# Clustered attention and an MLP on one core: the written order of all steps, its buffers and semaphores, made anew

## The chip, the cores and the metric

The kernel runs on one core of a Trainium2 chip. The metric is the time of one execution on the device in microseconds; the median of three runs is given, and beside it one execution that the hardware profiler recorded.

## The reference

q, k and v are float32 of shape 4 x 8 x 768 x 64 (batch, heads, sequence, head dimension). Every query and key is assigned to the nearest of 16 centroids of its head, and a query attends only to keys of its own cluster. The result, put together over the heads to 4 x 768 x 512, goes through a low-rank mix over the sequence and an MLP:

```python
mask = q_assign[:, :, :, None] == k_assign[:, :, None, :]
scores = np.where(mask, scale * np.matmul(q, k.transpose(0, 1, 3, 2)), -1000000000.0)
scores = scores - np.max(scores, axis=-1, keepdims=True)
attn = np.exp(scores)
attn = attn / (np.sum(attn, axis=-1, keepdims=True) + 1e-09)
x = np.matmul(attn, v)                      # heads side by side: 4 x 768 x 512
u = x + (x.transpose(0, 2, 1) @ U @ V).transpose(0, 2, 1)
out = u + np.maximum(u @ w_ch1, 0.0) @ w_ch2   # 512 -> 2048 -> 512
```

All is float32. The four arrays of weights come to the chip as 64-bit patterns that are joined to float32 there.

## The kernel before, in words

The work is cut into small steps, each a Python function that issues one to some ten instructions. list_work() lists them; a step marked @pieces(n) is a generator that is resumed n times. The list sequence (lines 93 to 300) says in which order the 4334 pieces are issued, and keep_order() (line 311) ties every instruction to the one before it on its engine and every DMA to the one before it of its queue, so this order is the program order of TensorE, DVE, ACT, POOL and of the DMA queues of SP and ACT. An instruction that must wait holds up all behind it on its engine. The dictionary kept (line 42) says for each kind of tile which of its buffers every new tile takes, in the order in which they are made ("w": the four PSUM banks of attention, "v" and "y": the two and six of the MLP, "pr": the eleven buffers of exponentials, "R": the two buffers of loaded queries and keys, later of u). The semaphores follow from both: the framework puts a wait wherever a tile is read after a write or a buffer is taken again.

Attention runs over i = 0 to 15 (batch, pair of heads). load (line 567), split_hi (656) and split_lo (671) cut queries and keys into a high and a low fp32r part in the arena; place_keys_hi, place_keys_lo, place_queries and place_clusters copy rows of it by DMA on SP's queue (helper copy_rows, line 441). rowmax multiplies (762) and DVE reduces (767); scores multiplies twice (793, 795) and ACT takes the exponential (799); weights sums exponentials on POOL or DVE (809); values multiplies by v in fp32 (817, o_ps). sums (832), sums_T (842) and normalise (855, 859) divide. For each batch mix_u (872), mix_sum (881 to 886) and mix_v (893 on TensorE, 895 on DVE) do the low-rank mix.

The MLP's first matrix product is done by a scheme of seven products for blocks (Strassen-Winograd); product(g, p) issues six fp32r matmuls (1081 to 1083) and its combination on DVE (1091) or ACT (1095). gemm2 (1284 to 1286) and finish (1293, 1296) do the second product for the first two batches, product2 (1228 to 1230), combine2 (1239) and output (1264 to 1274) for batches 2 and 3, where the second product is done by seven products too. In these two batches the weights are staged: stage_w(g, part) loads them on SP's queue (1168), split_staged casts the high part on ACT (1177) and subtracts on DVE or POOL (1175). fetch_blocks (1011) loads u in eight DMAs on SP's queue, turn_blocks (1017) transposes it, load_w2 loads pieces of the second weights on SP's queue (441).

Of the kernel before, what the change touches and what calls it, by code (L numbers as in the profile page):

```python
# [43 lines left out]
        "011010101010101010101010101010101010101010101010101011010011001010101010110101001",  # L44
    "rw":
        "0110101001011010101010101010101010010110010110010101",
    "rw_t":
        "0101010110010101001010101101010101010101010101010100101100110010110100110101010",
    "R":
        "0101011010101010100101101101100110",  # L50
    "pr":
        "0123456789a0213456890a21735468a9201735486a2017539486a2701539486a2071539486a0271539486a2071593486a0271593486a02"
        "71459386a20714589a620317459862307a1548962073a154896203a75148926073a5418692703a458169",
# [5 lines left out]
        "0101010101010101",  # L59
    "mT":  # L60
        "01010101010101010",
    "vt":
        "0120212011202120",
    "w":
        "01230312102323030021323112130121333220321030230123103213031001231203103212302130321201031203120313021023012310"
        "23120312301321321030231302120301131210321302131201031203120213013230130320320130231010230131201320210321301231"
        "02321032103120312231023012301201032012310231023013102323103123012310321203210132213021323211323201303312031031"
        "23012301231021020132012012303201210233012032103102313201201023012310231203103213123013121032010312303120321302"
        "02131230130321020213201231032130123012302103320210233231023210313012102302032130302203213102123102310310223132"
        "13213321201210321032132101233113201",  # L70
    "st":
        "01010101010101010101010101101010010101101001001010101011010100101010101010101011010101010101010101010110001001"
        "0101101101001010101011010101010110101010010101010101010101101010010101010101100101010101",
# [5 lines left out]
        "0101010101010101",  # L79
    "hh":  # L80
# [4 lines left out]
        "01010010101001010101010101011101010101010110100010011001101010100001001010100101111000110101010010101010100111"  # L85
        "011001010010110110010",
    "y":
        "01234523401552041342315450254132412314304102523513104245021340351042231524013250354510234054315214013054351343"
        "25404314204324512024350132403124530215041",
# [1426 lines left out]
```

## Time and profile before

| | us |
|---|---|
| median of 3 runs | 940.88 |
| the runs | 944.61, 940.88, 940.0 |
| the profiled execution | 937.66 |
| its span, first to last instruction | 935.9 |
| TensorE busy | 917.1 |
| DVE, POOL, ACT busy | 761.6, 660.9, 462.3 |

The span is what the trace covers; 1.8 us of the execution lie around it. A start time in the trace is counted from the span's first instruction. Matmuls are pipelined: the next one starts before the one ahead has ended, so the distance between starts, not the duration, is what one costs.

### The profile page before, as it was taken

Reading aid. Unit: us, or ns where it says so; the run is one execution under the profiler, and the core shown is the slowest. Engines: PE = TensorE matmul, PEld = TensorE weight load, DVE = VectorE, ACT = ScalarE, POOL = GpSimd, SP = SyncE. Lnnn points to the kernel's source line nnn. Section 1 sums busy time; section 2 is a strip of 40 time slices with the busy share of each in tenths; the row PEclk is TensorE's granted clock in tenths of the full one; section 3 lists DMA queues with packets and bytes.
Section 4 is the critical chain, followed back from the end, with each engine's and each line's share of the span. In section 5 each row is a group of like instructions: output and inputs, shape, how many; then the busy total and the mean of one; then the engine's idle time right before and its main releaser. Section 6 shows DMA issues by size and latency. Waiting matters only on the chain.

```text
span 935.9 us, 14676 instructions
## 1 busy us (share of the span) xinstructions
PE 917.1 (98%) x5098; PEld 742.5 (79%) x5098; DVE 761.6 (81%) x1255; ACT 462.3 (49%) x680; POOL 660.9 (71%) x433
## 2 busy tenths in 40 slices
PE   7999999999999999999999999999999999999997
PEld 5666666676676757665888888898889999999997
DVE  6999988878888888887988678877778878877785
ACT  7555555555655656465444344434344664255440
POOL 6478696798678899999999996875644773145520
PEclk9999999999999999999999999999999999999999
DMA  7765655566567756903578976558869879874887
GB/s 197 191 165 149 181 142 155 169 160 182 166 185 200 190 99 173 163 2 113 203 255 299 336 261 222 202 196 266 251 226 218 184 245 296 207 170 127 259 257 165
DMA packets 169645, 183.13 MB, mean 196 GB/s; under 512 B 110426, under 2 KB 119252, under 8 KB 168548
## 3 DMA queue, kind: packets, MB, share of 16 engines
q1 hardware_dynamic: 135072, 156.02, 59.5%
q10 hardware_dynamic: 34500, 26.19, 8.9%
q8 instruction: 40, 0.66, 0.3%
q14 instruction: 33, 0.27, 0.1%
HBM read 112.72 MB, written 41.42 MB: 165 GB/s over the span
## 4 chain that ended last, share of the span: by engine, by line
PE 84%; DVE 5%; DMA 5%; SPq 2%; POOL 1%; issue 1%; ACT 1%; ACTq 0%; DVEq 0%; POOLq 0%
PE o_ps L817 14%; PE ps_max L762 8%; PE st L793 7%; PE st L795 7%; PE ps_h L1081 6%; PE ps_h L1082 6%; PE ps_h L1083 6%; PE z L1228 4%; PE z L1229 4%; PE z L1230 4%; PE y L1286 4%; PE y L1285 4%; PE y L1284 4%; SPq L1011 2%; PE ps_sum L832 1%; PE ps_sim L578 1%
## 5 line engine op out<-in xcount | busy, mean ns | idle before, releaser
L809 POOL TENSOR_TENSOR T<-T,pr 128x768 f32<-128x768 f32 x120 | 226.7, 1897 | 28.0 <-ACT pr L799 13.0
L767 DVE TENSOR_REDUCE m<-ps_max 128x1 f32<-128x384 f32 x372 | 189.0, 548 | 42.9 <-PE ps_max L762 41.4
L799 ACT ACTIVATE pr<-st 128x768 f32<-128x768 f32 x186 | 147.9, 811 | 70.7 <-PE st L795 59.8
L817 PE MATMUL o_ps<-pr,vt 128*64 128x384 f32 x768 | 133.3, 492 | 0.0
L1081 PE MATMUL ps_h<-arena,combos 128*128 128x384 f32 x352 | 119.4, 339 | 1.1 <-DVE rw_g L1091 0.5
L1083 PE MATMUL ps_h<-arena,combos 128*128 128x384 f32 x352 | 118.2, 336 | 0.0
L1082 PE MATMUL ps_h<-arena,combos 128*128 128x384 f32 x352 | 118.1, 335 | 0.0
L762 PE MATMUL ps_max<-arena 128*128 128x384 f32 x372 | 111.0, 366 | 2.1 <-DVE m L767 1.7
L817 PEld LDWEIGHTS o_ps<-pr,vt 128*64 128x64 f32 x768 | 51.3, 136 | 67.5 <-issue 59.7
L793 PE MATMUL st<-arena 128*128 128x384 f32 x372 | 99.0, 347 | 0.0
L795 PE MATMUL st<-arena 97*128 97x384 f32 x372 | 95.4, 338 | 0.0
L762 PEld LDWEIGHTS ps_max<-arena 128*128 128x128 f32 x372 | 65.5, 188 | 37.6 <-DVE m L767 20.4
L809 POOL TENSOR_TENSOR T<-pr 128x768 f32<-128x768 f32 x30 | 56.5, 1883 | 47.8 <-ACT pr L799 35.4
L1286 PE MATMUL y<-w,hl 128*128 128x512 f32 x192 | 76.2, 397 | 0.8 <-DVE hl L1123 0.7
L1285 PE MATMUL y<-w,hh 128*128 128x512 f32 x192 | 75.7, 394 | 0.0
L1284 PE MATMUL y<-w,hh 128*128 128x512 f32 x192 | 74.7, 389 | 0.0
L1081 PEld LDWEIGHTS ps_h<-arena,combos 128*128 128x128 f32 x352 | 66.1, 188 | 9.1 <-DVE c L1091 2.4
L793 PEld LDWEIGHTS st<-arena 128*128 128x128 f32 x372 | 65.0, 189 | 10.2 <-issue 4.9
L1175 POOL TENSOR_TENSOR combos<-rw,combos 128x1024 fp32r<-128x1024 f32 x10 | 26.3, 2631 | 65.3 <-ACT combos L1177 31.8
L795 PEld LDWEIGHTS st<-arena 97*128 97x128 f32 x372 | 68.0, 189 | 0.1
L1082 PEld LDWEIGHTS ps_h<-arena,combos 128*128 128x128 f32 x352 | 66.1, 188 | 2.3
L1083 PEld LDWEIGHTS ps_h<-arena,combos 128*128 128x128 f32 x352 | 66.1, 188 | 0.3 <-DVE combos L1175 0.2
(214 smaller groups left out, 2079.9 us busy)
## 6 DMA issues: line engine op xcount, KB each, us to landing
combos<-w_scr SPq DMA_DIRECT2D x112, 256.0 KB
R<-in_qk SPq DMA_DIRECT2D x32, 384.0 KB
arena<-arena SPq DMA_DIRECT2D x64, 192.0 KB
arena<-arena SPq DMA_DIRECT2D x31, 384.0 KB
late_rw<-in_w SPq DMA_DIRECT2D x20, 512.0 KB
u<-u_scr SPq DMA_DIRECT2D x96, 96.0 KB
rw<-w_scr SPq DMA_DIRECT2D x15, 512.0 KB
vt<-in_v SPq DMA_DIRECT2D x16, 384.0 KB
```

Of the source, the lines that this page charges most:

```text
L762: nc.tensor.matmul(ps[:, 0:HS], x1[:, 0, g // 2, g % 2, t * P:(t + 1) * P], x1[:, 1, h, g % 2, :], start=True, stop=True)
L767: nc.vector.reduce_max(live["m2", i][:, h, u:u + 1], ps[:, 0:HS], axis=AX.X)
L793: nc.tensor.matmul(st[:, j, 0:HS], x1[:, 1, hk, j, ks], x1[:, 0, h, j, :], start=True, stop=False)
L795: nc.tensor.matmul(st[:, j, 0:HS], x2[0:97, 1, hk, j, ks], x2[0:97, 0, h, j, :], start=False, stop=True)
L799: nc.scalar.activation(pr, st[:, :, 0:HS], AF.Exp, scale=SCALE)
L809: eng.tensor_add(T, live["p", i, h, 0] if c == 1 else T, live["p", i, h, c])
L817: nc.tensor.matmul(o_ps[64 * j:64 * j + 64, 0:HS], vv[:, c, j, :], pr[:, j, :], start=(c == 0), stop=(c == NT - 1))
L1081: nc.tensor.matmul(ps, ah[:, d], oh[:, d], start=(d == 0), stop=False)
L1082: nc.tensor.matmul(ps, ah[:, d], ol[:, d], start=False, stop=False)
L1083: nc.tensor.matmul(ps, al[:, d], oh[:, d], start=False, stop=(d == 1))
L1285: nc.tensor.matmul(y, hh[:, f, ts], w2[:, 1, f, :], start=False, stop=False)
L1286: nc.tensor.matmul(y, hl[:, f, ts], w2[:, 0, f, :], start=False, stop=(g in lasts and f == 1))
```

## The change

The list sequence and ten of the strings in kept are replaced; "vt" and "st" also change their place in the dictionary. No function changes. The same 4334 pieces are issued in another order, and the tiles take other buffers, so the semaphores come out anew. The start of the diff:

```diff
     "rw_g":
-        "011010101010101010101010101010101010101010101010101011010011001010101010110101001",
+        "011010101010101100101010101010101010101010101010101011010011001010101010110101001",
...
     "R":
-        "0101011010101010100101101101100110",
+        "0101011010101010100110101101100110",
...
 sequence = [
-    0, 1, 12, 13, 14, 2, 3, 6, 4, 5, 16, 110, 9, 7, 107, 11, 10, 8, 15, 20, 18, 24, 26, 25, 117, 19, 108, 27, 21, 111, 41, 30,
...
```

The numbers say little, so here are the places that the prediction speaks of, as names of steps (function, arguments, and behind the point the piece), the old order left, the new one right. Other steps between them are left out.

```
# the start: SP's queue
load(1,0)                          load(1,0)
place_keys_lo(0)                   load(1,1)
load(1,1)                          place_keys_lo(0)
copy_keys                          copy_keys
place_ones(0)                      place_ones(0)
place_queries(0)                   place_ones(2)
place_keys_hi(1)                   place_queries(0)
place_ones(2)                      place_keys_hi(1)
place_keys_lo(1)                   place_ones(1)
load(2,0)                          place_keys_lo(1)
place_ones(1)                      load(2,0)
load(2,1)                          load(2,1)
place_queries(1)                   load_v(0)
place_clusters(1,0), (1,1)         place_queries(1)
load_v(0)                          place_clusters(1,0), (1,1)

# the last mix: TensorE (.0 of mix_v and product) and DVE (.1)
product(0,4).0                     product(0,4).0
mix_v(3,0).0                       mix_v(3,0).0
mix_v(3,0).1                       product(0,4).1
product(0,4).1                     mix_v(3,0).1
mix_v(3,2).0                       mix_v(3,1).0
mix_v(3,1).0                       mix_v(3,1).1
mix_v(3,2).1                       mix_v(3,2).0
mix_v(3,1).1                       mix_v(3,2).1

# batch 3 begins: SP's queue
stage_w(19,0)                      stage_w(19,0)
stage_w(19,1)                      finish(15,0).1
fetch_blocks(3,0)                  fetch_blocks(3,0)
finish(15,1).1                     stage_w(19,1)
stage_w(20,1)                      finish(15,1).1
stage_w(20,0)                      stage_w(20,0)
fetch_blocks(3,1)                  stage_w(20,1)
                                   fetch_blocks(3,1)

# batch 3, first products: SP's queue
stage_w(27,0)                      fetch_blocks(3,0)
fetch_blocks(3,0)                  stage_w(28,0)
stage_w(28,0)                      stage_w(27,0)
stage_w(27,1)                      stage_w(27,1)

# the end: TensorE, and the transfers that output issues from ACT
product2(3,5,6)                    output(3,4,1,2)
output(3,4,0,2)                    product2(3,5,6)
product2(3,6,2,1)                  output(3,4,0,2)
output(3,5,1,2)                    product2(3,6,3,1)
product2(3,6,5,0)                  output(3,5,0,2)
output(3,4,1,2)                    product2(3,6,4,1)
product2(3,6,4,1)                  output(3,5,1,2)
output(3,5,0,2)                    product2(3,6,5,1)
product2(3,6,5,1)                  product2(3,6,6,1)
product2(3,6,6,1)                  output(3,6,0,4)
output(3,6,0,4)                    product2(3,6,7,1)
product2(3,6,7,1)                  output(3,6,1,4)
output(3,6,1,4)
```

## Rows read from the trace of the kernel before

**Rows 1.** The page, part 1: busy us, share of the span, instructions.

```profile
PE 917.1 (98%) x5098; PEld 742.5 (79%) x5098; DVE 761.6 (81%) x1255; ACT 462.3 (49%) x680; POOL 660.9 (71%) x433
```

**Rows 2.** Windows: stretch, its length, busy us and instructions by engine, clock, DMA.

```profile
0.00:40.00 40.00, 32.02 (x196) 21.52 (x198) 29.39 (x67) 26.10 (x56) 24.55 (x64) 1.00 0.79 199
40.00:440.00 400.00, 398.99 (x2335) 267.67 (x2332) 342.11 (x647) 225.88 (x340) 328.74 (x179) 1.00 0.59 155
```

**Rows 3.** Waits of TensorE's matmuls: total us, times, longest.

```profile
PE ps_h L893 <- DVE xt L895: 1.3, 3, 0.8
```

**Rows 4.** Waits of TensorE's weight loads.

```profile
PEld ps_max L762 <- DVE m L767: 20.4, 42, 1.1
```

**Rows 5.** Groups by shape, TensorE: count, busy us, mean ns, idle before.

```profile
L762 PE MATMUL ps_max<-arena 128*128 128x384 f32 x372 | 111.0, 366 | 2.1 <-DVE m L767 1.7
L793 PE MATMUL st<-arena 128*128 128x384 f32 x372 | 99.0, 347 | 0.0
```

**Rows 6.** Chain that ended last, 60 to 112 us: start, us, what.

```profile
63.48 4.02 PE o_ps L817 x24
...
80.27 1.44 PE o_ps L817 x8
```

**Rows 7.** Timeline of DVE, 439.5 to 446 us: start, us, line, operation, tiles.

```profile
441.54 0.69 DVE L895 TENSOR_TENSOR xt<-ps_h,xt 128x512 f32<-128x512 f32 x1 [0.59 <-PE ps_h L893]
442.15 0.54 DVE L1091 TENSOR_TENSOR c<-rw_t,ps_h 128x384 f32<-128x384 f32 x1
442.82 3.27 DVE L895 TENSOR_TENSOR xt<-ps_h,xt 128x512 f32<-128x512 f32 x5
```

**Rows 8.** Timeline from 923.5 us: ACT's queue, SP's queue, DVE.

```profile
924.97 8.47 ACTq L1274 DMA_DIRECT2D out_y<-u  x16
...
929.23 3.61 SPq L1274 DMA_DIRECT2D out_y<-u  x4
...
930.73 0.56 DVE L1269 TENSOR_TENSOR u<-c,u 128x384 f32<-128x384 f32 x1
```

**Rows 9.** Timeline, 696 to 724 us: SP's queue, ACT, POOL, TensorE.

```profile
702.57 0.33 SPq L1168 DMA_DIRECT2D sums_w<-s_scr  x1
703.00 6.85 SPq L1011 DMA_DIRECT2D u<-u_scr  x8
...
711.15 0.39 SPq L1168 DMA_DIRECT2D rw<-w_scr  x1
...
712.56 1.04 ACT L1177 CAST combos<-sums_w 128x1024 fp32r<-128x1024 f32 x1
...
717.96 1.79 ACT L1177 CAST combos<-rw 128x768 fp32r<-128x768 f32 x2 [3.63 <-DMA rw<-w_scr]
...
713.67 2.63 POOL L1175 TENSOR_TENSOR combos<-sums_w,combos 128x1024 fp32r<-128x1024 f32 x1 [3.96 <-ACT combos L1177]
...
716.80 0.33 PE L1083 MATMUL ps_h<-operands,combos 128*128 128x384 f32 x1
716.98 0.33 PE L1081 MATMUL ps_h<-arena,combos 128*128 128x384 f32 x1
```

**Rows 10.** Timeline, 818 to 836 us: SP's queue, DVE, TensorE.

```profile
821.04 0.32 SPq L1168 DMA_DIRECT2D sums_w<-w_scr  x1
821.59 6.68 SPq L1011 DMA_DIRECT2D u<-u_scr  x8
...
829.50 0.34 SPq L1168 DMA_DIRECT2D rw<-s_scr  x1
...
830.97 0.95 DVE L1175 TENSOR_TENSOR combos<-sums_w,combos 128x768 fp32r<-128x768 f32 x1
...
833.39 0.33 PE L1081 MATMUL ps_h<-arena,combos 128*128 128x384 f32 x1
```

**Rows 11.** Chain that ended last, 819 to 837 us: a landing.

```profile
828.71 3.85 DMA rw<-w_scr
```

**Rows 12.** Chain that ended last, first 46 us: the transfer of place_queries(1).

```profile
24.32 5.51 DMA arena<-arena
```

More of the change, by code (lines that the diff above doesn't have):

```diff
@@ L43 @@
     "rw_g":
-        "011010101010101010101010101010101010101010101010101011010011001010101010110101001",
+        "011010101010101100101010101010101010101010101010101011010011001010101010110101001",
     "rw":
-        "0110101001011010101010101010101010010110010110010101",
+        "0101010110100101010110010101010101100101101001100101",
     "rw_t":
-        "0101010110010101001010101101010101010101010101010100101100110010110100110101010",
+        "0101010110010101001010101101010101010101010101010100101011001011001011010101010",
     "R":
-        "0101011010101010100101101101100110",
+        "0101011010101010100110101101100110",
     "pr":
-        "0123456789a0213456890a21735468a9201735486a2017539486a2701539486a2071539486a0271539486a2071593486a0271593486a02"
-        "71459386a20714589a620317459862307a1548962073a154896203a75148926073a5418692703a458169",
+        "0123456789a0123456890a21735468a9201735468a2071539846a2071539846a2071539486a0271593486a20715943860a127593486a02"
+        "71459386a207145986a20371458962037a1548962037a154896203a751489260735a418692703a451869",
     "mx":
@@ L59 @@
         "0101010101010101",
+    "vt":
+        "0120122011202120",
     "mT":
         "01010101010101010",
-    "vt":
-        "0120212011202120",
-    "w":
[L65 to L73, printed above, removed]
+    "w":
+        "01230312133220030021321133012121332322031302130022013310301301231032123012301230312021032103210313021023012310"
+        "23102313201321312030313202013120132130121302113201031230102123013302130323010230213012031031201230312021301321"
+        "02321031203120312320132102301201032012330120312013102323130123021310231230201312213021323231023112303231030131"
+        "23012031231021020132012032103210210233021032103012313201201203210301231203103123120313211032031023103210321032"
+        "01231230132010232013201231032130123021302103230213023230123201313012103202032130203201321021231230130321032131"
+        "22331321201230121302311201231310231",
     "T":
@@ L79 @@
         "0101010101010101",
+    "st":
+        "01010101010101010101010101101010010101101001001010101010110100101010101010101011010101010101010101010110001001"
+        "0101101101001010101011010101010110101010010101010101010101101010010101100101010101011001",
     "hh":
@@ L84 @@
     "v":
-        "01010010101001010101010101011101010101010110100010011001101010100001001010100101111000110101010010101010100111"
-        "011001010010110110010",
-    "y":
-        "01234523401552041342315450254132412314304102523513104245021340351042231524013250354510234054315214013054351343"
-        "25404314204324512024350132403124530215041",
+        "01010010101010100101010101011011010101010101010010100110101010010001001010100101110101001101010011001010010111"
+        "010110010101010101100",
+    "y":
+        "01234532410552401342132545041325412314034120531254130250421310435204231524013250351450420351432510431504531435"
+        "34023414204325420132041352403124530215014",
 }
 sequence = [
[207 rows of a table removed]
[207 rows of a table added]
 def pieces(n):
```

413 rows, old and new, of the table sequence are left out of this document.

## The prediction

> **What bounds the kernel now.** I read the page first: TensorE is busy 917.1 of 935.9 us [rows 1]. The program's matmuls are the same set in both kernels, so only the 18.8 us in which TensorE is not busy, and what is lost inside "busy", can change. The table of windows says where the first part lies [rows 2]: 8 us in the first 40 us, 1 us in the 400 us of attention. The waits of TensorE's matmuls name the rest: L893 on its DVE adds, 1.3 us [rows 3]. Inside "busy" the loss is read from the weight loads: before a row-maximum product (L762) they sat idle 20.4 us in 42 waits for the DVE reduce that frees the PSUM bank [rows 4]. The groups by shape price that from above: 372 products of L762 take 111.0 us and 372 of L793, the same shape, 99.0 us [rows 5], so 12.0 us are lost there, changes between fp32 and fp32r products among them. The new order can win or lose a part of these few microseconds; it has no large term.
>
> The profiled execution took 937.66 us with a span of 935.9, 1.8 us lying around it; the median of the three runs shown, 940.88, is 3.2 us above it. The sum below is a difference on the profiled execution, and I put the same difference on the median.
>
> **The change part by part.** I decoded both orders to step names and compared them engine by engine. Both hold the same 4334 pieces. On TensorE 736 of 1363 pieces keep their place and none moves by more than 7. No instruction is added or removed.
>
> *Fewer runs of fp32 products.* Products of o_ps, ps_sum, ps_sim, ps_xu and ps_rep are fp32, the others mostly fp32r. A run of 24 o_ps products takes 4.02 us and a run of 8 takes 1.44 [rows 6], so one product costs (4.02 - 1.44)/16 = 0.161 us, and 1.44 - 8 x 0.161 = 0.15 us belongs to the run itself. What leaving the run costs isn't in that piece; the upper bound is twice it, 0.3. The new order has 63 such runs where the old has 67. I take 0.2: **-0.8 us**, bounds -0.6 and -1.2.
>
> *The last mix (L893, L895).* The adds of mix_v(3) run back to back on DVE and TensorE waits for them: 0.69 us for the first, five more in 3.27, and the combination of product(0,4) (L1091, 0.54 us) sits between the first and the rest [rows 7]. In the new order that combination stands ahead of the first add, where DVE would wait for the matmul anyway. If its matmul is finished by then the chain is shorter by the whole instruction and the gap around it, 442.82 - (441.54 + 0.69) = 0.59 us; if not, by nothing. Between 0 and -0.6 I take **-0.6**, since product(0,4) is issued ahead of mix_v(3,0) in both orders.
>
> *The tail.* The last add ends at 930.73 + 0.56 = 931.29 [rows 8]. ACT issues sixteen output transfers without a break from 924.97 to 933.44, 0.53 us each, so the last two, which could be issued by 931.29 + 2 x 0.53 = 932.35, end 1.1 us later; SP's last ends at 932.84 [rows 8]. The new order issues the four of output(3,4,1,2) earlier, behind product2(3,5,5), out of this queue. The gain is between 0.6 (SP unchanged) and 1.1: **-0.8**. Their cover is the products of p = 6, which last until 930.
>
> *The start.* load_v(0) moves ahead of place_queries(1) on SP's queue, load(1,1) moves from behind place_keys_lo(0) to the front. The transfer of place_queries takes 5.51 us [rows 12] and what is behind it waits. One load is put ahead of it and one of the same size (768 fp32 a partition) goes from ahead of it to the front, so the bytes to move before it are the same. Bounds: one such load each way; as two loads are issued just ahead of this transfer in the old order, I put one at a third of the row, 1.8 us (an estimate from [rows 12]). I take **0**.
>
> *Staged weight loads.* This is where the new order is tighter. SP's queue is in order. (a) stage_w(19,1) was issued at 702.57, just ahead of the eight issues of fetch_blocks(3,0), which hold SP for 6.85 us [rows 9]; it now stands behind them, so it goes out at about 709.4. In that stretch one staged load issued at 711.15 kept ACT waiting until 717.96, 6.8 us [rows 9]; another, at 828.71, landed in 3.85 [rows 11]. With 3.85 the load is there at 713.3, the cast of 1.04 and POOL's subtraction of 2.63 [rows 9] make it 716.9, and the product that needs it started at 716.98 [rows 9]: hidden. With 6.8 it is 2.8 us late. (b) stage_w(27,0) was issued at 821.04, ahead of fetch_blocks(3,0) (6.68 us); it now stands behind it and behind stage_w(28,0), about where an issue at 829.50 stood [rows 10]. Landing 3.85 later, with a cast of 0.78 (1.04 [rows 9] for 768 instead of 1024 columns) and DVE's 0.95, it is ready at 835.1, and its product started at 833.39: 1.7 us late. But SP had waited until 821.04 for the buffer of (27,0), so fetch_blocks can start earlier and give the 1.7 back. Behind both waits stand the other steps of SP's queue, fetch_blocks(3,1) and stage_w(28,1), and behind ACT's casts its activations. For each I take the value of the nearer landing with the earlier start, **0**; the ends 0 and 2.8, 0 and 1.7 go into the range.
>
> On (a) the Trainium skill has a rule that speaks against the change: "DMA: Bandwidth & Descriptors", "Queues, rings and completion order", says that descriptors on a DMA engine are consumed in ring order. By it the staged load always waits for the small pieces of the fetch ahead, and the sum would be +0.6 instead of -2.2; the 6.8 us row agrees with it, the 3.85 us row, also issued just behind such a fetch, does not show as much.
>
> Sum: -0.8 - 0.6 - 0.8 + 0 + 0 = **-2.2 us**. The profiled execution would be 935.5 and the median 940.88 - 2.2 = **938.7**.
>
> **The rivals.** *Staged loads land late (slower).* Place: ACT's casts (L1177) behind fetch_blocks, 705 to 840 us. Price: 2.8 + 1.7 = 4.5, less 2.2, that is +2.3: 943.2. The order shows more of it: counted in products of 1.04 us (six matmuls at the 0.17 us between starts [rows 9]) the lead of (20,1) falls from 9.4 to 5.2 and of (30,1) from 7.3 to 4.2. If these two also lose 2.8 each the time is 948.8. It decides from a landing of about 4 us. For it: the 6.8 us row. Against it: ACT is idle for 3.63 us ahead of that very cast [rows 9] and TensorE did not stop there.
>
> *Bank waits shrink (faster).* An order that bears delays should leave more work between the reduce that frees a bank and the product that takes it. If half of the 12.0 us of rows 5 goes, the time is 938.7 - 6 = 932.7. Against it speaks the count: row-maximum products with under 0.75 us of matmul work between are 148 in the old order and 148 in the new; for it, the o_ps runs that start with under 0.25 us fall from 10 to 3, and the runs shown lie up to 944.61 - 937.66 = 6.95 us above the profiled one, which small delays may cause.
>
> Beside it: the Trainium skill, "TensorE: Matmul & The Clock Gate", "Step-by-step: what each phase is for", says that weight loads are pulled ahead of running matmuls. Were that always so these waits would cost nothing and this case would be empty; the 20.4 us disagree.
>
> *Nothing happens.* The displacements are small and TensorE's start and tail stay: 940.9. For it speaks that the named gains are each under 1 us.
>
> **How the numbers follow.** A measurement of this kernel can tell about 0.5%, 4.7 us, from no change: 936.2 and 945.6 are the bounds. Forecast 0.42 (all but 0.07 of it above 936.2), bank waits 0.28 (nearly all faster), late staged loads 0.18 (two thirds above 945.6, where more than two places are late), nothing 0.12. Faster 0.34, same 0.53, slower 0.13. The range goes from the bank case, 932.7, taken a little lower, to a little above the two-place case of 943.2: 932.0 to 944.5.
>
> **What would show it.** The end of ACT's issues no more than 1.1 us behind the last add; no L1091 between the adds of L895 at 442; the o_ps chain pieces as long as now. Wrong would be: TensorE waits for casts (L1177) near 717 or 834, or a weight-load idle for L767 far from 20.4 us.

## The result, and the profile after

The new kernel takes 950.09 us (median of 15 executions, 943.84 to 955.66) against 941.65 (15 executions, 940.0 to 944.93) of the old one run beside it: the ratio is 1.0088, interval 1.0068 to 1.0109, **slower by 0.9%**. The forecast was 938.7 with a range up to 944.5: the sign is wrong and the range doesn't hold the result. The executions also lie further apart, 11.8 us against 4.9; but the 13 to 27 executions of the old kernel beside the experiments spread over 7.8 to 9.9 us, so this says little. TensorE's clock goes with a part of the difference: the mean granted clock is 0.9945 over the 15 executions, against 0.9963 over 19 executions of the old kernel beside the first experiments, and 0.0018 of 950 us is 1.7 us (an estimate from these two means). The rest has to be found in the trace. The profiled execution took 951.49 us with a span of 949.7.

Part 1 of the page and the windows of the new kernel answer to [rows 1, 2] (busy us and instructions by engine, clock, DMA):

```profile
PE 920.9 (97%) x5098; PEld 742.3 (78%) x5098; DVE 771.2 (81%) x1255; ACT 462.9 (49%) x680; POOL 659.7 (69%) x433
```

```profile
0.00:40.00 40.00, 32.09 (x190) 20.62 (x192) 29.15 (x66) 26.20 (x56) 24.54 (x64) 1.00 0.73 185
40.00:440.00 400.00, 393.24 (x2305) 263.31 (x2300) 342.18 (x640) 224.30 (x336) 321.74 (x175) 1.00 0.61 154
```

The stretch of attention is where to look: TensorE idles for 6.8 of its 400 us instead of 1.0, and starts 30 products fewer in it. The waits of TensorE's matmuls say for what (total us, times, longest). Of these lines only L1081 and L762 behind DVE stood there before, with 0.7 and 1.7 us; the three DMA lines are new. The lines cover the whole execution: 5.2 of the 6.3 us of L1081 lie in the MLP, between 440 and 720 us, and 3.6 of the 5.4 us of the DMA lines in attention, between 40 and 440:

```profile
PE ps_h L1081 <- DVE c L1091: 6.3, 6, 2.0
PE st L795 <- DMA arena<-mT: 2.9, 4, 1.5
PE ps_max L762 <- DVE m L767: 2.6, 4, 1.4
...
PE ps_max L762 <- DMA arena<-ohT: 1.6, 3, 1.0
...
PE ps_sumT L842 <- DMA rw<-in_V: 0.9, 1, 0.9
```

The weight loads behind [rows 4] and the groups behind [rows 5] moved little:

```profile
PEld ps_max L762 <- DVE m L767: 17.7, 32, 1.7
```

```profile
L762 PE MATMUL ps_max<-arena 128*128 128x384 f32 x372 | 111.8, 368 | 5.0 <-DVE m L767 2.6 <-DMA arena<-ohT 1.6 <-DVE m L772 0.4
L793 PE MATMUL st<-arena 128*128 128x384 f32 x372 | 99.1, 347 | 0.0
```

The chain of waits names the places in attention (start, us, what). Read it as a list of causes: a small transfer of ACT that lands after 5.01 us; SP held for 1.3 us by a load (L567), with the transfer that TensorE needs behind it; a copy of ohT behind that same kind of load; and two subtractions of DVE that take 7.49 us:

```profile
59.12 5.01 DMA arena<-mT
66.03 1.32 SPq L567
...
69.21 3.15 DMA rw<-in_V
```

```profile
195.40 1.15 SPq L567
...
199.17 3.58 DMA arena<-ohT
```

```profile
393.38 7.49 DVE arena L1031 x2
```

The last mix answers to [rows 7], the tail to [rows 8], both timelines:

```profile
448.20 0.55 DVE L1091 TENSOR_TENSOR c<-rw_t,ps_h 128x384 f32<-128x384 f32 x1
448.77 3.27 DVE L895 TENSOR_TENSOR xt<-ps_h,xt 128x512 f32<-128x512 f32 x5
452.82 0.69 DVE L895 TENSOR_TENSOR xt<-ps_h,xt 128x512 f32<-128x512 f32 x1 [0.78 <-PE ps_h L893]
```

```profile
936.96 9.88 ACTq L1274 DMA_DIRECT2D out_y<-u  x14
```

```profile
944.38 2.40 SPq L1274 DMA_DIRECT2D out_y<-u  x4
```

```profile
945.36 0.56 DVE L1269 TENSOR_TENSOR u<-c,u 128x384 f32<-128x384 f32 x1
```

The combination stands ahead of the adds now, as the change says, but the sixth add waits 0.78 us for its product; from the first add's start to the last one's end it is 4.74 us, against 4.55 before. In the tail ACT's issues end at 946.84 and SP's at 946.78, 0.9 us behind the last add instead of 2.15.

### The profile page after: what moved, and what is told of

It is laid out like the page before. It is cut to its first block, busy times and chain, and to the rows that moved or that the text cites. A ratio compares the mean times of both kernels' runs of the same rounds, so it can differ in the third digit from the quotient of the medians.

```text
span 949.7 us, 14665 instructions
## 1 busy us (share of the span) xinstructions
PE 920.9 (97%) x5098; PEld 742.3 (78%) x5098; DVE 771.2 (81%) x1255; ACT 462.9 (49%) x680; POOL 659.7 (69%) x433
## 4 chain that ended last, share of the span: by engine, by line
PE 70%; DMA 10%; DVE 8%; POOL 4%; issue 3%; ACT 2%; SPq 2%; ACTq 1%; DVEq 0%; POOLq 0%
PE o_ps L817 11%; PE ps_max L762 7%; PE ps_h L1081 6%; PE st L793 6%; PE st L795 6%; PE ps_h L1083 6%; PE ps_h L1082 6%; PE z L1228 4%; PE z L1230 4%; PE z L1229 4%; PE y L1286 2%; PE y L1285 2%; PE y L1284 2%; DMA s_scr<-sums_w 2%; DMA combos<-w_scr 2%
## 5 line engine op out<-in xcount | busy, mean ns | idle before, releaser
L809 POOL TENSOR_TENSOR T<-T,pr 128x768 f32<-128x768 f32 x120 | 227.0, 1900 | 38.5 <-ACT pr L799 20.7
L1081 PE MATMUL ps_h<-arena,combos 128*128 128x384 f32 x352 | 120.6, 343 | 4.1 <-DVE c L1091 3.9
L762 PE MATMUL ps_max<-arena 128*128 128x384 f32 x372 | 111.8, 368 | 5.0 <-DVE m L767 2.6
L795 PE MATMUL st<-arena 97*128 97x384 f32 x372 | 95.8, 338 | 2.9 <-DMA arena<-mT 2.9
L762 PEld LDWEIGHTS ps_max<-arena 128*128 128x128 f32 x372 | 65.3, 188 | 41.9 <-DVE m L767 17.7
L1081 PEld LDWEIGHTS ps_h<-arena,combos 128*128 128x128 f32 x352 | 66.6, 189 | 13.6 <-DVE c L1091 8.4
L1175 POOL TENSOR_TENSOR combos<-rw,combos 128x1024 fp32r<-128x1024 f32 x10 | 24.2, 2423 | 69.3 <-DMA out_y<-u 26.2
L795 PEld LDWEIGHTS st<-arena 97*128 97x128 f32 x372 | 67.8, 189 | 4.2 <-DMA arena<-mT 4.2
```

The lines of the kernel that those rows point to most:

```text
L762: nc.tensor.matmul(ps[:, 0:HS], x1[:, 0, g // 2, g % 2, t * P:(t + 1) * P], x1[:, 1, h, g % 2, :], start=True, stop=True)
L795: nc.tensor.matmul(st[:, j, 0:HS], x2[0:97, 1, hk, j, ks], x2[0:97, 0, h, j, :], start=False, stop=True)
L809: eng.tensor_add(T, live["p", i, h, 0] if c == 1 else T, live["p", i, h, c])
L1081: nc.tensor.matmul(ps, ah[:, d], oh[:, d], start=(d == 0), stop=False)
```

## The experiments

At 194 places both orders have issued exactly the same set of pieces. There one order can be left and the other taken up, with the buffers carried over, so a stretch can be swapped and nothing else. To compare traces I took the start of TensorE's first instruction behind such a place, counted in program order, and subtracted the old trace's: "late at piece n". The table behind the last experiment has these numbers for every run.

**Which stretch.** Three kernels, each the old one with one stretch in the new order:

```diff
 att:   -pieces 1 to 2432 old      +pieces 1 to 2432 new
 mlp:   -pieces 2433 to 3419 old   +pieces 2433 to 3419 new
 last:  -pieces 3420 to 4334 old   +pieces 3420 to 4334 new
```

> The new order for the first 2432 pieces (all of attention up to about 536 us), the old order behind them. Theory A, local stalls: the trace of the new kernel is 8.7 us late at this cut against the trace of the old one, 13.8 us at the end, and the medians are 8.5 us apart; so this kernel is 5 to 8.7 us slower than the old one. Rival B, staged loads of batch 3: nothing here, within 1 us of the old time. Rival C, the new order only spreads more, wherever it stands: 0 to 5 us, with runs further apart than the old kernel's.

> The new order for pieces 2433 to 3419 alone (the MLP of the first two batches, about 536 to 705 us), the old one ahead and behind. Theory A, local stalls: the trace lost 5.7 us there, so 3 to 5.7 us slower than the old kernel. Rival B, staged loads: within 1 us of the old time. Rival C as for the attention: 0 to 3 us and more spread.

> The new order for the last 915 pieces alone (batches 2 and 3 with staged weights, from about 705 us). Theory A: the trace lost 0.2 us up to the last stretch and won 0.8 in the tail, so -1 to +0.5 us. Rival B, staged loads land late: +2.3 to +8 us, as the prediction's slower case had it, and TensorE waits near 717 and 834 us. Rival C: 0 to 3 us and more spread.

att: 951.9 us, ratio 1.0114 (1.0068 to 1.016), which is 10.7 us and more than the 8.7 that theory A allowed. mlp: 1.0006 (0.9982 to 1.0029). last: 1.0009 (0.9986 to 1.0032). All of the loss comes with attention; the new order of the MLP and of batches 2 and 3, staged loads and tail included, costs nothing that can be measured (the intervals reach 0.3%). That is the end of the slower rival of the prediction. The MLP's share was a miss: the new kernel's trace lost 5.7 us there, yet the new MLP alone costs nothing, while att, whose MLP has the old order, loses 5.8 us in it.

**One small transfer.** The new kernel with one step moved:

```diff
-place_keys_lo(3)  ... 26 pieces ...  rowmax_place(1,6,12).2
+rowmax_place(1,6,12).2  place_keys_lo(3)
```

> The new kernel with one piece moved: place_keys_lo(3), two copies on SP's queue, goes from 26 pieces ahead of the transfer of rowmax_place(1,6,12), which ACT issues, to directly behind it, as in the old order. Theory A1, that large copies issued ahead of it on another queue make the small transfer late: the wait of L795 on it near 64 us (1.6 us in the new kernel, none in the old) is gone or under 0.4 us. Rival A2, that the transfer is slow by itself or that ACT's order makes it late: the wait stays at 1 to 1.6 us.

The wait is gone: no wait of L795 near 64 us. From ACT's issue to the end of the transfer's last packet it was 3.76 us in the new kernel, and is 1.41 here, as in the old one (1.41). A1 holds for this place. The kernel as a whole took 956.7 us. That is one execution, and its longest wait, 3.67 us for L1091 at 684 us, lies in the MLP, so this time tells nothing of the repair. Another wait, for rw<-in_V, stood at 71 us with 1.4 us (0.9 in the new kernel).

**The loads in front.** Seven steps of SP's queue moved back in the new kernel (loads_back), the same with one subtraction of DVE moved (loads_split_back), and the mirror image in the old kernel (loads_ahead):

```diff
 loads_back, in the new order:
-load(9,1)  place_queries(8)  place_clusters(8,0)
+place_queries(8)  place_clusters(8,0)  load(9,1)
...
 loads_ahead, in the old order:
-place_queries(8)  place_clusters(8,0)  load(9,1)
+load(9,1)  place_queries(8)  place_clusters(8,0)
```

> The new kernel with seven steps of SP's queue in attention moved behind the small copies that TensorE waits for, as in the old order: place_keys_lo(3) behind the transfer of rowmax_place(1,6,12); load(5,1) behind load_v(2); load(4,0) behind load_mix(2,0); load(6,1) behind the transfer of rowmax_place(3,0,12); load_v(8) and place_ones(7) behind place_clusters(7,1); load(9,1) behind place_clusters(8,0). Theory A1, large transfers ahead of small ones: TensorE's waits near 64, 72, 103, 176 and 202 us, 3.9 us together in the new kernel's trace, fall below 1 us, and the time by 2 to 4 us against the new kernel's 950.1, to 946 to 948. Rival A2, the order of the work on TensorE, DVE and ACT: these waits stay in sum above 2.5 us and the time within 1.5 us of 950.

> The same, and one piece of DVE moved: the subtraction of split_u(0,b21) goes ahead of values(13,1,0) and so ahead of the reduce of rowmax(15,5,0), so that the two subtractions L1031 near 393 us don't stand back to back. In the new kernel's trace the first of them took 6.7 us, while POOL worked without a pause for 6.1 of them, and TensorE lost 1.6 us at 401. Theory D, DVE's subtraction is held by POOL's work: with another alignment it takes 1 to 2.6 us, the wait at 401 falls under 0.5 us, and the time is 1 to 2 us below the other repaired kernel. Rival: the pair of subtractions keeps 7 us and the wait stays, as POOL's work is the same.

> The mirror image: the old kernel with such steps moved ahead of the small copies, as the new order has them: place_keys_lo(3) directly behind load(4,0); load(5,1) ahead of place_clusters(3,0); load(6,1) ahead of rowmax_place(3,0,12); load_v(8) and place_ones(7) ahead of place_queries(7); load(9,1) ahead of place_queries(8). Theory A1: TensorE gets waits on the transfers of mT and ohT near 63, 103 and 200 us that the old kernel has not, 2 to 4 us together, and the kernel is 2 to 4 us slower than the old one. Rival A2: no such waits, within 1 us of the old kernel.

Times: 1.0112 (1.0051 to 1.0174), 1.0103 (1.0052 to 1.0153), 1.0008 (0.9976 to 1.004). As totals they speak against A1: undoing did not help, and doing did not hurt beyond an interval that reaches 1.004. But loads_back can't decide it by its total, since one of its moves brought a loss of its own. At 66 us of the old order's time its TensorE stands 0.2 us ahead of the old trace, where the new kernel's is 2.5 late; at 75 us it is 5.6 late (new kernel 3.6); and from there to 438 us it loses only 0.7 us more, the new kernel 3.6. Place by place, then, most of the undoing worked. At 176 and 202 us the waits went in loads_back, and the mirror image made one, the longest of its attention, with SP's queue just ahead of it (load(9,1) holds the queue for 1.49 us, then the copies). In order, TensorE's timeline and SP's:

```profile
201.18 0.41 PE L762 MATMUL ps_max<-arena 128*128 128x384 f32 x1 [2.37 <-DMA arena<-ohT]
```

```profile
192.75 1.49 SPq L567 DMA_DIRECT2D R<-in_qk  x1
194.28 1.14 SPq L441 DMA_DIRECT2D arena<-arena  x2
195.47 2.61 SPq L441 DMA_DIRECT2D arena<-ohT  x4
```

At 103 the wait did not go (0.2 us in the new kernel, 0.5 here), since moving load(6,1) past a step of ACT doesn't hold SP: a place in the written order binds only within a queue. At 72 it became worse, and that shows the real cause there. I had moved load(4,0) still later, to 3 pieces ahead of its cast, and ACT's cast of it stands at the head of ACT's queue, ahead of the copy of o_ps that TensorE waits for. The new kernel's cast, then that of loads_back and what TensorE does:

```profile
71.08 0.83 ACT L656 CAST arena<-R 128x768 fp32r<-128x768 f32 x1 [4.31 <-DMA R<-in_qk]
```

```profile
71.59 0.83 ACT L656 CAST arena<-R 128x768 fp32r<-128x768 f32 x1 [7.69 <-DMA R<-in_qk]
```

```profile
72.86 0.68 PE L842 MATMUL ps_sumT<-ident,sums 128*128 128x128 f32 x3 [4.13 <-ACT os L823]
```

The subtraction: the pair takes 2.35 us in loads_back already, without the move, and TensorE's wait at 401 is gone in both. The same instruction, started a little later against POOL's work, so this fits theory D's alignment, though the move was not what brought it. DVE's timelines of the old kernel, the new one and loads_back:

```profile
387.12 2.53 DVE L1031 TENSOR_TENSOR arena<-turned,arena 128x768 fp32r<-128x768 f32 x1 [0.61 <-ACT arena L1029]
...
390.04 2.10 DVE L1031 TENSOR_TENSOR arena<-turned,arena 128x768 fp32r<-128x768 f32 x1
```

```profile
393.30 7.57 DVE L1031 TENSOR_TENSOR arena<-turned,arena 128x768 fp32r<-128x768 f32 x2
```

```profile
394.37 2.35 DVE L1031 TENSOR_TENSOR arena<-turned,arena 128x768 fp32r<-128x768 f32 x2
```

**Half of attention.** The new order for 1420 pieces:

```diff
 half1: -pieces 1 to 1420 old   +pieces 1 to 1420 new
```

> The new order for the first 1420 pieces alone (to about 254 us), the old one behind. The kernel with all of the attention in the new order was 11.5 us slower than the old one: its trace stood 4.7 us behind at this cut, 9.1 us at the end of attention, and lost 5 us more in the MLP, whose order was the old one. Theory A, local stalls, with the loss in the MLP caused by the second half: 3 to 5 us slower. Rival E, any disturbance ahead lets the MLP lose its few us too: 7 to 10 us slower, and drift grows by 3 to 5 us behind 470 us.

1.0128 (1.0068 to 1.0189): the whole loss comes with the first 1420 pieces. And rival E looks right in its numbers: 6.7 us late at the cut, 8.1 at the end of attention, 14.2 behind the MLP, in an order that is the old one from 254 us on. But loads_ahead was 3.5 us late at the cut as well, and its MLP lost only 1.0.

**What carries it into the MLP.** Behind piece 1420 half1 differs from the old kernel in one thing, the two buffers rw are swapped. Four kernels:

```diff
 rw_swap:   -rw "0110101001..."   +rw "1001010110..."     (old kernel)
 half1_rw:  half1 with rw swapped back
 start:     -pieces 1 to 391 old     +pieces 1 to 391 new
 second:    -pieces 392 to 1420 old  +pieces 392 to 1420 new
```

> The old kernel with nothing moved: only the two buffers of raw weights (rw) change names throughout. In the kernel with the new order for its first 1420 pieces, this swap is the only thing that differs from the old kernel behind piece 1420, and yet its MLP lost 5.4 us there. Theory G, the loss hangs on which of the two buffers a load takes: 3 to 6 us slower, with waits of L1081 for DVE's combinations near 480 and 505 us. Rival H, the loss hangs on when things happen: within 1.5 us of the old kernel, no such waits.

> The kernel with the new order for its first 1420 pieces (+12 us), with the buffers rw swapped back, so that everything behind piece 1420 is the old kernel to the letter. Theory G: the MLP's 5.4 us go, 5 to 8 us slower than the old kernel remain. Rival H: as slow as before the swap, 10 to 13 us.

> The new order for the first 391 pieces alone (to about 70 us), the old one behind; the buffers rw are swapped behind it, as they come out of the new start. The trace of the kernel with 1420 new pieces stood 3.4 us behind at this cut. Theory A, local stalls: 3 to 4 us slower than the old one. Theory G: the MLP loses its 4 to 5 us too, 7 to 9 us. Rival: the start costs nothing in most executions, within 2 us.

> The new order for pieces 392 to 1420 alone (70 to 254 us), with the buffers rw as in the old kernel. The trace of the kernel with 1420 new pieces lost 3.3 us there, at 103, 176, 203, 247 and 257 us. Theory A, local stalls: 3 to 4 us slower than the old one. Theory G: no more than that, since rw is not swapped. Rival E, that any order but the old one lets the MLP lose some: 7 to 9 us.

rw_swap: 0.9993 (0.9974 to 1.0012). half1_rw: 1.0084 (1.0057 to 1.0111). start: 1.0053 (1.0031 to 1.0074). second: 1.0076 (1.0052 to 1.01). The buffers don't matter, G falls: half1_rw's time alone would fit it, but its MLP loses 5.7 us all the same. These two kernels also show how far one trace can be trusted: half1 and half1_rw issue the same pieces in the same order up to 1420, and stand 6.7 and 2.6 us late there. Both halves of the first 1420 pieces are slow for themselves, and start is a clear case: it is 1.0 us late at piece 1420 and 2.5 at the end of attention, and then loses 5.5 us in an MLP of the old order. The five kernels with an early change of this kind (att, half1, half1_rw, start, second) wait at the same two places there, 1.6 and 1.0 to 1.3 us for L1091.

What they share was found among the DMA packets. The page's list of queues has one of instructions: 40 packets of 16 KB, and TensorE's 10,395 records over 40 are 260 each, so I take it for the fetches of TensorE's program.

```profile
q8 instruction: 40, 0.66, 0.3%
```

Put on the old kernel's time, which is good to about 0.7 us, one fetch comes at 481.9 to 482.9 us in the old kernel, last, loads_ahead and rw_swap, and at 475.5 to 476.0 in the five slow ones. At 476.6 ACT issues w_scr<-turned. And the five have two to five semaphore waits more in TensorE's program by then than the old kernel's 144, while last and rw_swap have 144 and loads_ahead 140. So theory F: the number of instructions ahead sets when a fetch comes, and a fetch on top of a DMA issue delays it, with ACT's cast, DVE's in-order queue and TensorE behind.

**Instructions added and taken away.** Nothing moved, only transposes into an unused bank in the first microseconds:

```diff
 spin_more, the old kernel:
-*((spin, k, 2 if k > 1 else 4) for k in range(21))
+*((spin, k, 2 if k > 1 else 5) for k in range(21))
 half1_spin, after_spin (half1_rw and the new kernel):
-*((spin, k, 2 if k > 1 else 4) for k in range(21))
+*((spin, k, 2 if k > 1 else 2) for k in range(21))
```

> The old kernel with two transposes more on TensorE in its first microseconds (spin(0) and spin(1) write five instead of four into their unused bank), which are four instructions more in TensorE's program; every step, buffer and wait behind them is the old kernel's. Theory F: TensorE's program is fetched 16 KB at a time, and a fetch that falls on a DMA issue holds that issue up by about a microsecond. In the five kernels whose MLP lost 5 us the fetch near 476 us of the old kernel's time meets ACT's issue of w_scr<-turned, with two to five waits more ahead of it in TensorE's program; in those that lost 1 to 2.6 us it comes 6 us later. So here the fetch comes at 476, ACT's issue takes 0.9 to 1.5 us instead of 0.45, TensorE waits about 1.8 us for L1091 soon after, and the kernel is 3 to 5 us slower. Rival H, it hangs on when things happen in attention: within 1 us of the old kernel.

> The kernel with the new order for its first 1420 pieces and the old one behind to the letter (+9.4 us), with four transposes fewer in spin(0) and spin(1), which are eight instructions fewer in TensorE's program, so that it has by 452 us three instructions fewer than the old kernel instead of five more. Theory F: the fetch near 476 is back at 482, the waits near 486 and 510 go, the MLP loses 0 to 2.5 us instead of 5.7, and the kernel is 3 to 5 us faster than with the transposes, at 945 to 948. Rival H: it stays at 949 to 952.

> The new kernel itself with the same four transposes fewer. Theory F: its MLP lost 5.9 us against the old kernel's trace, the new order of the MLP behind the old attention 1.8; with the fetches moved the time falls by 2 to 4 us, to 946 to 948. Rival H: 949 to 951 as before.

spin_more: 1.004 (1.0017 to 1.0063), 3.8 us (2.8 between the medians), by four instructions. half1_spin: 948.55, 1.0057 (1.0028 to 1.0087), where half1_rw had 950.67 and 1.0084; the intervals overlap. after_spin: 1.0088 (1.0064 to 1.0111), as the new kernel. In all three the fetch went where F had put it (476.4, 482.2, 482.3). The two kernels with the old MLP moved as forecast in direction; spin_more lost 3.7 us in the MLP, though in its trace ACT's issue kept its 0.45 us: it began 0.14 us ahead of the fetch, where in the five slow kernels it began 0.04 to 0.51 us behind the fetch's start. Its waits stood at 494 and behind 550. At 494 the chain is another one: ACT's late_g waits 4.17 us for a load of late_rw, which is read 6.3 us after its issue instead of 3.7. The waits behind 550 stand in rw_swap too, which is not slower. In the new kernel the trace's MLP did lose 0.4 us instead of 5.7, and the median did not follow: for the new kernel itself F is not shown to decide. In its trace no issue of w_scr<-turned near 480 is lengthened (0.33 us), and its longest waits for L1091 stand at 595 and 676 us, 1.3 and 2.0 us, with no cause shown here.

**One load, and the named places together.** load4_late is the old kernel with a shorter lead for load(4,0). repaired is the new one with the old start and four places undone; repaired_spin is that with the fetch moved:

```diff
 load4_late, in the old order:
-load(4,0)  ... 65 pieces ...  split_hi(4,0)
+load(4,0)  ... 13 pieces ...  split_hi(4,0)
 repaired, in the new order:
-pieces 1 to 391 new
+pieces 1 to 391 old
-load_v(4)  load(6,1)  place_keys_hi(5)
+place_keys_hi(5)  load_v(4)  load(6,1)
...
```

> The old kernel with one step moved: load(4,0), the first half of the fifth pair, goes from 65 pieces ahead of its cast split_hi(4,0) to 15 pieces ahead of it, behind place_clusters(3,0) and load_mix(0,1) on SP's queue; the new order has it 18 ahead. Theory A3, ACT's cast waits at the head of its queue for that load and holds the copy of o_ps that TensorE waits for: an idle of 2 to 6 us ahead of the cast L656 near 68 us (none in the old kernel's trace) and 0.4 to 2 us of TensorE waiting for L823 near 70; the kernel 0.4 to 2 us slower. Rival: the load lands in time, no wait, same time.

> The new kernel with its first 391 pieces in the old order and, behind them, four places of attention undone: load_v(4) and load(6,1) behind place_keys_hi(5); load_v(8) and place_ones(7) behind place_clusters(7,1); load(9,1) behind place_clusters(8,0); the subtraction of split_u(0,b21) ahead of values(13,1,0). The rest (most of the pieces behind 391, the last mix, the MLP, the tail) is the new order. Theory A, local stalls each with its own cause: the waits near 64, 72, 103, 202 and 401 us, 5.4 us together in the new kernel's trace, fall to under 1.5 together, and the time from 950.1 to 944 to 947. Rival: other waits take their place, 948 to 951.

> The same with four transposes fewer in spin(0) and spin(1), which are eight instructions fewer in TensorE's program. Theory F, fetches: if the fetch near 476 us falls on ACT's issue in the kernel above and not here, this one is 2 to 4 us faster, at 942 to 945; if it falls on it in neither, the two are within 1.5 us. Rival H: the transposes matter by themselves, slower by up to 1 us.

load4_late: 1.0035 (1.0011 to 1.0058). The load stands 13 pieces ahead of its cast, not 15 as the expectation has it. ACT does wait for the load, 3.04 us ahead of the cast, but no product waits near 70 us: attention took up the delay. The kernel is slower for another reason, and it is F's cleanest case. It has one wait more on TensorE (145), the fetch comes at 476.0, ACT's issue takes 1.33 us, the cast behind it and late_g come 0.9 us later, DVE's L394, which reads late_g, takes 1.90 us instead of 0.45 beside an instruction of POOL that has started by then, and TensorE waits. ACT's timeline of the old kernel, ACT's of load4_late, TensorE's of load4_late:

```profile
476.64 0.45 ACTq L441 DMA_DIRECT2D w_scr<-turned  x1
477.19 0.84 ACT L1056 CAST combos<-rw 128x768 fp32r<-128x768 f32 x1 [1.86 <-PE ps_h L1083]
```

```profile
478.82 1.33 ACTq L441 DMA_DIRECT2D w_scr<-turned  x1
480.25 0.84 ACT L1056 CAST combos<-rw 128x768 fp32r<-128x768 f32 x1 [2.75 <-issue]
```

```profile
484.12 0.45 PE L1081 MATMUL ps_h<-arena,combos 128*128 128x384 f32 x1 [1.60 <-DVE c L1091]
```

repaired: 1.0126 (1.0089 to 1.0163), repaired_spin: 1.0106 (1.0075 to 1.0136). F has a fetch on the issue in neither, and the two medians, 2.5 us apart, are not told apart by their intervals. The waits near 64, 72, 103 and 202 us are gone, and the kernel is no faster. Others took their place, one of my own making (values of pair 4 reach load_v(4), which I had put 45 pieces later than the new order and 51 later than the old one), and the subtraction met POOL again, 7.23 us, though it stood alone. TensorE's timeline, then DVE's:

```profile
116.42 2.19 PE L817 MATMUL o_ps<-pr,vt 128*64 128x384 f32 x6 [2.66 <-DMA vt<-in_v]
...
399.68 1.33 PE L762 MATMUL ps_max<-arena 128*128 128x384 f32 x3 [2.73 <-DVE m L767]
```

```profile
391.92 7.23 DVE L1031 TENSOR_TENSOR arena<-turned,arena 128x768 fp32r<-128x768 f32 x1
```

How late TensorE is against the old trace, in us, at places of the old order's time, shows what the repairs did:

| kernel | 66 | 75 | 112 | 121 | 240 | 391 | 403 | 438 | 452 |
|---|---|---|---|---|---|---|---|---|---|
| last (old order here) | 0.2 | 0.2 | 0.2 | 0.2 | 0.2 | 0.1 | 0.1 | 0.1 | 2.5 |
| the new kernel | 2.5 | 3.6 | 3.6 | 3.4 | 4.8 | 5.5 | 7.4 | 7.2 | 8.7 |
| loads_back | -0.2 | 5.6 | 5.5 | 5.3 | 5.5 | 6.6 | 6.5 | 6.3 | 7.7 |
| repaired | 0.7 | 0.6 | -0.5 | 3.7 | 4.1 | 4.6 | 8.8 | 10.1 | 12.4 |

Up to 112 us repaired had made good the new kernel's whole loss. Then it lost 4.2 us at the load that I had put later, and 4.2 at the subtraction (391 to 403). loads_back lost 5.8 us at load(4,0) and nothing at the subtraction. So these two times don't say that the loss can't be undone; each repair brought a loss of its own. The last column holds a loss that is not the order's: last, with the old order, loses 2.4 us there too.

**All runs.** "Late" is TensorE in the profiled execution against the old kernel's, at pieces 1420 (254 us), 2432 (452) and 3419 (716); "more" the instructions in TensorE's program ahead of piece 2432 beyond the old kernel's; "fetch" the one near 480, in the old kernel's time. keys_back was run once. Each row is one execution: half1_rw, start, after_spin and loads_back were recorded 2.9 to 5.6 us below their medians, the old kernel itself, at 937.66, 2.7 to 5.1 below its medians of 940.4 to 942.8 beside the experiments.

| kernel | ratio | late at 1420 | 2432 | 3419 | in the MLP | more | fetch |
|---|---|---|---|---|---|---|---|
| *the old MLP* | | | | | | | |
| last | 1.0009 | 0.1 | 2.5 | 3.4 | 0.9 | 0 | 482.0 |
| rw_swap | 0.9993 | -0.1 | 1.5 | 4.1 | 2.6 | 0 | 481.9 |
| loads_ahead | 1.0008 | 3.5 | 4.9 | 5.9 | 1.0 | -4 | 482.9 |
| half1_spin | 1.0057 | 5.7 | 8.1 | 10.7 | 2.6 | -3 | 482.2 |
| load4_late | 1.0035 | -0.4 | 2.2 | 7.4 | 5.2 | 1 | 476.0 |
| start | 1.0053 | 1.0 | 2.5 | 8.0 | 5.5 | 2 | 476.0 |
| second | 1.0076 | 6.5 | 8.6 | 14.9 | 6.3 | 3 | 476.0 |
| spin_more | 1.0040 | 0.8 | 2.0 | 5.7 | 3.7 | 4 | 476.4 |
| att | 1.0114 | 4.7 | 9.1 | 14.9 | 5.8 | 4 | 475.6 |
| half1_rw | 1.0084 | 2.6 | 3.8 | 9.5 | 5.7 | 5 | 475.5 |
| half1 | 1.0128 | 6.7 | 8.1 | 14.2 | 6.1 | 5 | 475.6 |
| *the new MLP* | | | | | | | |
| mlp | 1.0006 | 0.5 | 1.7 | 4.4 | 2.7 | 0 | 482.5 |
| the new kernel | 1.0088 | 5.3 | 8.7 | 14.4 | 5.7 | 4 | 478.8 |
| keys_back | | 6.2 | 12.7 | 20.7 | 8.0 | 4 | 476.8 |
| loads_back | 1.0112 | 6.6 | 7.7 | 12.7 | 5.0 | 4 | 479.0 |
| loads_split_back | 1.0103 | 6.8 | 8.0 | 13.4 | 5.4 | 4 | 477.1 |
| after_spin | 1.0088 | 5.9 | 10.2 | 10.6 | 0.4 | -4 | 482.3 |
| repaired | 1.0126 | 4.5 | 12.4 | 13.2 | 0.8 | 0 | 479.7 |
| repaired_spin | 1.0106 | 6.1 | 11.4 | 13.5 | 2.1 | -8 | 482.5 |

Two columns carry the reading. Among the eleven kernels with the old MLP, the seven with any instruction more have the fetch at 475.5 to 476.4 and lose 3.7 to 6.3 us in the MLP; the four with none more have it at 481.9 to 482.9 and lose 0.9 to 2.6. The column "late at 2432" goes with pieces 392 to 1420: where they are in the new order it is 3.8 to 12.7, elsewhere 1.5 to 4.9. In every row 1.2 to 2.5 us of it arose between 438 and 452 us, where TensorE's clock fell in all of these traces and not in the old kernel's; that much is the luck of the one old trace.

The column "in the MLP" can be cut in two. From 452 to 512 us the six kernels with a lengthened issue (0.93 to 1.54 us: the five and load4_late) lose 3.1 to 3.4 us, spin_more 1.9, and the four with none more less than 0.1. From 512 to 716 us the six lose 2.1 to 3.1 us, and the four with none more 0.8 to 2.7. So some 3 us go with the lengthened issue; the rest is lost by kernels that are not slower as well. One place is left that the experiments did not touch: near 256 us a product of L762 waits 0.9 to 1.5 us for DVE's add L895 in nine of the twelve kernels with pieces 392 to 1420 new, and in none of the others.

## Why the prediction was wrong

**The step that failed** is the first: "The new order can win or lose a part of these few microseconds; it has no large term." I read the idle and lost time of the old trace as the room of the change in both directions. It bounds what an order can win. What it can lose is bounded by nothing in the old trace: there attention had 1 us of waits [rows 2] because every landing came in time, and I did not measure by how much. The new kernel's attention has 6.8.

**The start** I costed at 0, with 1.8 us each way, from one transfer. start alone costs 0.53%, 5.0 us: 1.0 by piece 1420, most of the rest in the MLP, by a road that I did not have: "No instruction is added or removed" leaves out the semaphore waits, of which TensorE's program has four more ahead of piece 2432 in the new kernel, and two more in start. And I stopped at the loads in front of place_queries(1): the lead of load(4,0) over its cast, which falls from 65 pieces to 18, stands 200 pieces further on, and leads of transfers in attention were compared nowhere in the prediction.

**Fewer runs of fp32 products**, -0.8: not seen. The L762 products stayed at 111.8 us against 111.0, and no run isolates the term. **The last mix**, -0.6: the gap went as described, and another of 0.78 us stands before the sixth add; the choice of the full value was the mistake, 0 the measured one. **The tail**, -0.8: right. From the last add's end to the span's end it is 3.75 us instead of 4.61, so -0.9. **Staged weight loads**, 0: right in both places. The new order's cast of (19,1) waited 0.26 us, for TensorE, and last, which has all of these steps, is within 0.3% of the old kernel.

Of the rivals, late staged loads were the wrong landing: the landings that came late are in attention, small copies and load(4,0). Bank waits did shrink, to 17.7 us from 20.4, and it won nothing. What I put down as a sign for that rival, that the runs of the old kernel spread by 6.95 us, was a sign of how far its executions lie apart; whether the new order spreads more is open.

**Shown and open.** Shown: the new order of the first 1420 pieces alone costs the whole loss; four instructions added on TensorE in unused time, and nothing else, make the old kernel 0.4% slower; copies ahead of a small transfer make it late at 64 us (keys_back) and at 202 us (loads_ahead), by one trace of each. Read from the traces, one execution each: most of what the new kernel loses in attention stands at places with a cause named (64 and 72 us, together 2.7 us; the subtraction, 1.9), and loads_back and repaired made these losses good where they did not bring others; no run undoes them all without a loss of its own. Of the MLP's loss, some 3 us go with an issue that meets a fetch, in six traces of kernels with the old MLP. That the meeting is how the added instructions cost time is only argued, since spin_more is slower by as much with that issue undisturbed. Open: the wait near 256 us, and what the new kernel's own MLP waits for. No kernel here beats the old one.

## What to carry to other kernels

An order in which TensorE hardly ever waits tells nothing of how far it is from waiting: before such an order is redone, compare for both the lead of every transfer over its first reader, by queue, and what stands behind that reader on its engine. When a stretch gets slower whose code did not change, compare what comes from outside it (instructions ahead on each engine, when fetches fall, where two engines share a port) before looking for a cause in the stretch. And test a repair in the whole kernel, with its trace laid beside the old one: here the waits went and the time stayed, because each repair had moved another transfer too close to its reader.

## What the runs showed of the hardware

**A few instructions more can cost 0.4%.** With four instructions of transposes added, or with one wait more, a 16 KB fetch of TensorE's program came 6 us earlier and the kernel took 0.40 and 0.35% longer. In load4_late an ACT issue that met it took 1.33 us instead of 0.45; why spin_more is slower is not shown. The Trainium skill, "Runtime: NRT & Kernel Launch", "Instruction fetch mechanics", has the engine's program refilled in blocks of 16 KB and calls the cost of crossing such a boundary mostly hidden. The size agrees with the 40 packets here; the cost was not hidden from the issue that it met.

**DVE can starve beside POOL.** The subtraction L1031 of 128 x 768 took 0.95 us where it met no work of POOL, and 6.70 in the new kernel, while POOL ran four instructions of 0.76 to 1.88 us one after the other. The Trainium skill, "SBUF — State Buffer", "SBUF: two separate sides", describes one port pair shared by the two as an exclusive lock, held for a whole instruction by whoever starts first. The trace fits this in part: POOL's three long instructions took 1.85 to 1.88 us, about as long as those before them, and DVE ended 0.8 us behind the last one. But DVE lost to several instructions of POOL in a row, and in loads_back, started 0.1 us ahead of POOL's short one, it took 0.95 us while that one took 1.45 instead of 0.76.

**The clock falls behind the last mix.** In the window of 440 to 480 us, just after the stretch in which TensorE waits for the six adds, the granted clock was 1.00 in the old kernel's trace and 0.96 in the new one's, so part of that window ran at 1.2 instead of 2.4 GHz. The two rows:

```profile
440.00:480.00 40.00, 38.22 (x185) 32.62 (x184) 34.92 (x44) 18.68 (x25) 37.57 (x25) 1.00 0.51 177
440.00:480.00 40.00, 37.95 (x177) 30.29 (x176) 31.48 (x42) 17.19 (x24) 36.81 (x25) 0.96 0.45 151
```

last, whose order is the old one there, had 0.91, and lost 2.4 us at this place. All 19 other traces have such a fall there, with either order, and the old kernel's is the one without; so it does not come from the new order. A long wait elsewhere can cost the same way: in loads_back, behind the wait of 4.13 us at 72 us, the granted clock was 0.88 between 66 and 80 us, where the new kernel's was 1.00.
